# A transformer block on one core: another fixed order for the same instructions

## The chip, the cores and the metric

The kernel runs on one core of one Trainium2 chip. A core has five engines that share no clock and meet only at semaphores: TensorE (PE in the profile: matmuls; PEld: its weight loads), VectorE (DVE), ScalarE (ACT), GpSimd (POOL) and SyncE (SP), which here only issues DMAs. Each engine works off its own list of instructions in order. The metric is the time of one execution on the device in microseconds, the median of the runs.

## The reference

A pre-norm block on 2048 tokens of width 640: an attention with a compressive memory, then a feed-forward layer of width 1728.

```python
h = x + _A_ref(_layernorm(x, axis=-1), A_wq, A_wk, A_wv, A_wo, A_beta)
h2 = h + _B_ref(_layernorm(h, axis=-1), B_w1, B_w2)      # silu between the two products
...
for s in range(N):                                        # N = 4 segments of L = 512 tokens
    logits = jnp.einsum('bhqd,bhkd->bhqk', qs, ks) * scale + mask
    p = _softmax(logits, axis=-1)
    a_dot = jnp.einsum('bhqk,bhkd->bhqd', p, vs)
    num = jnp.einsum('bhld,bhde->bhle', phi(qs), M)
    den = jnp.einsum('bhld,bhd->bhl', phi(qs), z)[..., None] + 1e-06
    o = g * num / den + (1.0 - g) * a_dot
    M = M + jnp.einsum('bhld,bhle->bhde', phi(ks), vs)
    z = z + jnp.einsum('bhld->bhd', phi(ks))
```

There are 32 heads of 20 columns each. phi(t) is t + 1 for positive t and exp(t) otherwise.

## The kernel before, in words

The work is cut into four segments of 512 tokens, and each segment into tasks of one to twenty instructions. `build` declares every task with the buffers that it reads and writes and the engines that may run it. The order is not computed: a long text, `ORDER` (from L356), names every task once, and `Graph.schedule` walks it word by word. A word is `name/engine:slots`. The engine is A, D, G or S for ACT, DVE, POOL or SyncE, where the task may run on more than one; the slots are the buffers that the task is the first to use, in PSUM the first of its banks (there are eight, of 512 columns in float32). The instructions of one engine run in the order of the words. `Tracker.add` puts in the semaphore waits that reads, writes and reused buffers need. So the text fixes three things: the order on every engine, the engine of every evacuation out of PSUM, and which task reuses whose buffer.

The names, for segment s, group g of heads, column c of the projection (five of them; w = 0 for q, 1 for k):

- `x4`, `w_w1_0`: loads of tokens and weights. `re_wq0`, `re_wk0`: copies of weight columns into a padded layout (L693 on ACT, L695 on DVE).
- `n1_st`, `n1_r`, `n1_ap`: layer norm of a block of 128 tokens (statistics L743 on DVE, power L764 on POOL, scaling L770 on DVE). `n1_tp`/`n1_te`: its transpose on PE and the evacuation, for the first four blocks; `n1_tr`: the same by a DMA transpose (L799), for all others. `n2_...`: the second norm.
- `pr010x`: projection, segment 0, c = 1, w = 0, first half of the tokens (x; y is the second half) (PE, L867, the first ones L872). `qe010x`: its evacuation (ACT L883 or DVE L884). `v03`, `ve03`: V projection of a block (PE L828) and its evacuation (ACT, or DVE L843).
- `ex021`, `pha021`, `phb021`: phi, an exp on ACT (L890) and two steps on DVE (L897, L903). `kt02`, `kg02`: transpose of phi(k) by DMA and its gather. `mz10`, `ma10`: the memory's product (PE, L1226) and its addition to M (DVE L1242, in segment 0 an evacuation). `zf0`, `lsc0`: small exps of beta on ACT.
- `vt02`: copy of a part of q and k from SBUF to SBUF by DMA (L915). The five projected columns hold five groups of four heads and, in their unused rows, pieces of three more groups; twelve such copies for each segment, the virtual-head copies, put the pieces together. `vp13`: the same for phi(q). Both may be issued from SyncE's queue or from ACT's.
- `qk4x10`: scores of four heads at a time (PE, L965) into four PSUM banks. `e4x1+`: their exp on ACT in one instruction of 2048 columns (L977); `e4x30`, `e4x32` are two of 1024. `mk...`: the causal mask on POOL (L988).
- `av0x`, `oe0x`, `tn0x`, `nm0x`, `ad8`: attention times V (PE, L1093 in segment 0 and L1009 later), evacuation, transposition back (PE), normalisation on DVE, sum on POOL. `ot1`, `wo1`, `rs1`: transpose by DMA, output product (PE, L1273), residual on DVE (L1281).
- `h1_0_7_0`, `th`, `s`: first feed-forward product (PE, L1308), tanh (ACT, L1317), product (DVE, L1323). `h2_0_1`, `o0`, `out0`: second product (PE, L1350), residual (DVE, L1363), store.

The scores of the last three groups of heads (g = 5, 6, 7) read the virtual-head copies. In segment 0 `qk4x10` is the first such task: it packs group 4 with a piece of group 5, and so waits for all twelve copies `vt00` to `vt011`; `vt00`, `vt03`, `vt06` and `vt09` need columns 0, 1 and 2, the other eight columns 3 and 4. Each `vt` waits for its evacuations on the queue that issues it, and whatever comes later in that queue waits behind it.

```python
ORDER = """
...
""".split()
...
t.eng = {"A": AC, "D": DV, "G": PO, "S": SP}[eng] if eng else list(t.engs)[0]
...
virt(3 * r, allq((0, 1, 2)), QKV_[p:p + 12, :, :, :], QK_[p + 20:p + 32, 0:3, :, :])
virt(3 * r + 1, allq((3, 4)), QKV_[p + 12:p + 20, 0:2, :, :], QK_[p + 20:p + 28, 3:5, :, :])
virt(3 * r + 2, allq((3, 4)), QKV_[p + 12:p + 20, 2, :, :], QK_[p + 28:p + 32, 3:5, :, :])
```

Of the kernel before, what the change touches and what calls it, by code (L numbers as in the profile page):

```python
# [1426 lines left out]
```

## Time and profile before

| what | before |
|---|---|
| median of 3 runs | 296.63 us (296.54 to 297.4) |
| profiled execution, span from the first to the last instruction | 296.3 us (no other time is given for it) |
| ACT, DVE, POOL busy | 217.3, 222.2, 140.0 us |
| granted TensorE clock | 1.000 |
| DMA, mean over the span | 86 GB/s |
| exps of the scores on ACT (L977, 120 instructions) | 153.2 us |

A profile line of one instruction or a run of alike ones has the start in us, the length in us, the engine, the line of the code, the operation, what is written and read with its shape, the count, and in brackets the engine's idle time just before with what ended it. SPq and ACTq are DMA issues. A tile name can be that of the memory under it: segment 0 keeps its q and k in the space of `w_sb`, so its projections' evacuations and virtual-head copies read `w_sb<-ps_all` and `w_sb<-w_sb`, later segments' read QK and QKV.

### The profile page before, as it was taken

The page shows a single profiled execution, that of the slowest core. Times are in us where ns is not written, and L with a number is a line of the kernel's source. Part 1 is how long each engine was busy: PE and PEld are TensorE (multiplying, and loading weights), DVE is VectorE, ACT ScalarE, POOL GpSimd, SP SyncE. Part 2 cuts the span into 40 slices and gives each one's busy share as a digit, 9 for nine tenths or more (in the row PEclk, how much of TensorE's full clock was granted, in tenths as well). Part 3 has the DMA queues.
Part 4 walks back from the last instruction along what each step waited for, and adds up shares of the span by engine and source line. Part 5 has one row for each costly group of instructions (what it writes and reads, how often), then busy time and mean ns, then how long its engine had stood idle before and what let it go on. Part 6 is the DMA issues. An engine that isn't in the chain of part 4 may idle for free.

```text
span 296.3 us, 7415 instructions
## 1 busy us (share of the span) xinstructions
PE 282.1 (95%) x2968; PEld 167.6 (57%) x2991; DVE 222.2 (75%) x506; ACT 217.3 (73%) x266; POOL 140.0 (47%) x257
## 2 busy tenths in 40 slices
...
GB/s 243 367 173 105 173 133 71 221 18 75 189 94 74 53 60 22 40 109 106 104 96 61 66 1 2 27 76 87 22 99 32 0 61 74 68 67 25 22 22 91
DMA packets 49922, 25.40 MB, mean 86 GB/s; under 512 B 39504, under 2 KB 48048, under 8 KB 49888
## 3 DMA queue, kind: packets, MB, share of 16 engines
...
## 4 chain that ended last, share of the span: by engine, by line
PE 78%; DVE 8%; DMA 6%; issue 2%; ACT 2%; SPq 1%; POOL 1%; DVEq 0%; ACTq 0%
PE ps_all L1350 19%; PE ps_all L1308 17%; PE ps_all L867 12%; PE ps_all L965 7%; PE ps_all L1273 6%; PE ps_all L828 5%; PE ps_all L1009 5%; DMA x_tok<-in_A_x_dram 3%; DMA xT<-xn_rot 2%; ACT PT L977 2%; PE ps_all L1039 1%; DVE stt L743 1%; PE ps_all L1093 1%; DMA w_sb<-w_sb 1%; PE ps_all L1226 1%
## 5 line engine op out<-in xcount | busy, mean ns | idle before, releaser
L977 ACT ACTIVATE PT<-ps_all 128x1024 bf16<-128x1024 f32 (+1 forms) x120 | 153.2, 1310 | 16.9 <-PE ps_all L965 15.7
L988 POOL TENSOR_SCALAR_AFFINE_SELECT PT<-PT 128x512 bf16<-128x512 bf16 x128 | 81.6, 648 | 59.2 <-ACT PT L977 56.9
L1350 PE MATMUL ps_all<-w_sb,sT 128*128 128x320 bf16 (+2 forms) x462 | 64.9, 295 | 0.0
L1308 PE MATMUL ps_all<-hT,w_sb 128*128 128x512 bf16 (+1 forms) x315 | 61.0, 336 | 1.2 <-issue 0.6
L1317 ACT ACTIVATE th<-ps_all 128x512 f32<-128x512 f32 (+2 forms) x70 | 34.1, 505 | 35.3 <-PE ps_all L1308 31.2
L1350 PEld LDWEIGHTS ps_all<-w_sb,sT 128*128 128x128 bf16 x462 | 43.2, 98 | 18.3 <-issue 1.8
L1323 DVE SCALAR_TENSOR_TENSOR sT<-th,ps_all 128x512 bf16<-128x512 f32 (+2 forms) x70 | 37.9, 561 | 17.8 <-ACT th L1317 16.9
L1308 PEld LDWEIGHTS ps_all<-hT,w_sb 128*128 128x128 bf16 x325 | 29.9, 98 | 25.3 <-issue 3.5
L764 POOL TENSOR_TENSOR rst<-rst,eps_c 128x1 f32<-128x1 f32 x32 | 18.3, 576 | 24.4 <-DVE rst L758 23.1
L743 DVE BATCH_NORM_STATS2 stt<-x_tok 128x6 f32<-128x320 bf16 x62 | 27.2, 481 | 1.1 <-DMA x_tok<-in_A_x_dram 0.7
L1363 DVE SCALAR_TENSOR_TENSOR x_tok<-ps_all,x_tok 128x640 bf16<-128x640 f32 (+3 forms) x18 | 13.3, 745 | 16.7 <-PE ps_all L1350 16.6
L1071 POOL TENSOR_TENSOR otok<-on 128x320 bf16<-128x320 bf16 x24 | 19.0, 797 | 11.7 <-DVE on L1063 11.7
L1273 PE MATMUL ps_all<-wo_sb,oT 128*128 128x320 bf16 x160 | 23.8, 299 | 0.0
L884 DVE CAST QK<-ps_all 128x512 bf16<-128x512 f32 x23 | 15.7, 688 | 9.1 <-PE ps_all L867 8.9
L1063 DVE TENSOR_TENSOR on<-ps_all,rd 128x640 bf16<-128x640 f32 x24 | 19.8, 824 | 0.9
L828 PE MATMUL ps_all<-wv_sb,xT 128*128 128x320 bf16 x120 | 18.3, 299 | 1.1 <-DMA xT<-xn_rot 0.9
L1273 PEld LDWEIGHTS ps_all<-wo_sb,oT 128*128 128x128 bf16 x160 | 15.0, 98 | 7.2 <-issue 1.8
L867 PE MATMUL ps_all<-xT,wkr 128*128 128x512 bf16 x67 | 16.9, 379 | 1.2 <-issue 0.8
L867 PE MATMUL ps_all<-xT,wqr 128*128 128x512 bf16 x70 | 17.3, 380 | 0.4 <-issue 0.2
L1009 PE MATMUL ps_all<-PT,Vx 128*32 128x512 bf16 (+3 forms) x384 | 16.4, 301 | 0.1
L843 DVE CAST Vx<-ps_all 128x640 bf16<-128x640 f32 x15 | 12.3, 818 | 5.4 <-PE ps_all L828 5.3
L770 DVE TENSOR_SCALAR xn_rot<-x_tok,mvt,rst 128x640 bf16<-128x640 bf16 x32 | 14.9, 475 | 1.7 <-POOL rst L764 1.0
...
## 6 DMA issues: line engine op xcount, KB each, us to landing
...
```

Source lines behind the costliest of these rows:

```text
L743: T.add(DV, lambda e, hh=hh: e.bn_stats(out=stt[:, s, 6 * hh:6 * hh + 6], in_=xb[:, 320 * hh:320 * hh + 320]), reads=R((xa, xsub)), writes ...
L828: fns.append(lambda e, c=c, hh=hh: e.matmul(bank(ps, hh)[:, 0:320], lhsT=xT_[:, c, 128 * i:128 * i + 128], rhs=wv_sb[:, c, 320 * hh:320 * ...
L867: fns = [lambda e, kc=kc: e.matmul(bank(ps)[:, lo:hi], lhsT=wt[:, kc, c, :], rhs=xT_[:, kc, lo:hi], start=(kc == 0), stop=(kc == NC - 1)) ...
L965: fns.append(lambda e, j=j, o=o, r=r, q0=q0, q1=q1, qa=qa, ka=ka: e.matmul(ps_all[:, o:o + q1 - q0], lhsT=ka[32 * r:32 * r + DH, 128 * j:1 ...
L977: T.add(AC, lambda e: e.activation(out=pt[:, pta.slot, q0:q0 + nq, 0:width], in_=sc3[:, b0:b0 + nq, 0:width], func=ACT.Exp, scale=SCALE), ...
L988: T.add(PO, lambda e: e.affine_select(out=v, in_=v, pattern=[[0, 4], [1, 128]], compare_op=ALU.is_ge, fill=0.0, base=0, channel_multiplier ...
L1009: fns.append(lambda e, j=j, r=r, h=h, pa=pa, pt=pt, co=co, q0=q0, ji=ji: e.matmul(bank(po)[32 * r:32 * r + 32, q0:hi], lhsT=Vx[:, vx.slot, ...
L1273: fns.append(lambda e, c=c, hh=hh: e.matmul(bank(ps, hh)[:, 0:320], lhsT=oT[:, c, 128 * i:128 * i + 128], rhs=wo_sb[:, c, 320 * hh:320 * h ...
L1308: fns = [lambda e, c=c: e.matmul(bank(ps)[:, lo:hi], lhsT=w1_sb[:, c, 128 * f:128 * f + 128], rhs=hT[:, c, lo:hi], start=(c == 0), stop=(c ...
L1317: T.add(AC, lambda e: e.activation(out=th[:, tha.slot, lo:hi], in_=bank(ps)[:, lo:hi], func=ACT.Tanh, scale=0.5), reads=R((ps, [0])), writ ...
L1323: T.add(DV, lambda e: e.scalar_tensor_tensor(out=sT[:, f, lo:hi], in0=th[:, tha.slot, lo:hi], scalar=1.0, in1=bank(ps)[:, lo:hi], op0=ALU. ...
L1350: fns.append(lambda e, f=f, t0=t0, fr=fr, hh=hh, n=n: e.matmul(bank(pa, hh)[:, 0:n], lhsT=sT[:, f, t0:t0 + 128], rhs=w2_sb[:, fr, c0 + 320 ...
```

## The change

Only the text `ORDER` changes. It names the same tasks, 383 words on PE in both. On PE the order differs mainly in the first projections and scores and, at the end, in the last segment's feed-forward; in between some twenty near neighbours are swapped. On the other engines more is moved. Counted over both lists, these tasks changed their number on an engine:

| tasks | before | after |
|---|---|---|
| ve (V evacuation) | ACT 1, DVE 15 | ACT 5, DVE 11 |
| oe (attention evacuation) | ACT 9, DVE 23 | ACT 11, DVE 21 |
| qe (projection evacuation) | ACT 18, DVE 32 | ACT 19, DVE 31 |
| re_wq | ACT 1, DVE 4 | ACT 2, DVE 3 |
| ma (memory evacuation) | ACT 1, DVE 8 | DVE 9 |
| vt (virtual-head copies of q, k) | ACT 6, SyncE 42 | ACT 18, SyncE 30 |
| vp (of phi(q)) | ACT 3, SyncE 33 | ACT 11, SyncE 25 |
| out (stores) | ACT 10, SyncE 8 | ACT 13, SyncE 5 |
| kg, kh (gathers) | DVE 8, POOL 13 | DVE 9, POOL 12 |
| n1_r, n2_r (step one of the power) | DVE 16, POOL 16 | DVE 13, POOL 19 |

In segment 0 each list issues four of the twelve `vt` from ACT: before `vt07`, `vt010`, `vt00`, `vt03`, now `vt04`, `vt011`, `vt03`, `vt06`. The diff, cut to the part up to the output products wo1 and wo0 (minus lines, then plus lines), the stretch around `rs2` and `mz10`, and the end:

```diff
-epsg0:0 vpad0 zpad w2z/G:0 fill30:7 x0:0 w_q1:0 warm iota mt mta mtb mm7 x1:4 mm0 n1_st1/A:0,0 w_q0 w_q2 epsc sel
+epsg0:0 vpad0 zpad w2z/G:0 fill30:7 x0:10 w_q1:0 warm iota mt mta mtb mm7 x1:4 mm0 n1_st1/A:0,0 w_q0 w_q2 epsc sel
 halfc n1_st0/D:5 n1_r0/G n1_r1/D n1_ap0:0 n1_tp0:4 n1_te0a/A:0 n1_ap1:1 n1_tp1:0 n1_te0b/A n1_te1b/D n1_te1a/A w_k0
-re_wq1/D:0 pr010x:4 re_wq4/A re_wq2/D pr020x:2 qe020x/A:0 qe010x/A:0 re_wq3/D re_wq0/D pr000x:5 pr040x:6 w_k1
-re_wk2/A:0 qe000x/A:0 re_wk1/D qe040x/A:0 pr011x:0 qe011x/A re_wk0/D pr001x:2 pr021x:5 qe001x/A qe021x/A x2:10,5
-n1_st2/D:3 n1_r2/G qk0x10:0 pr030x:7 w_wv0:0 w_wv1 n1_st3/D:1 n1_r3/G e0x10:4 x4:2,1,11,3 qe030x/A:0 w_wo:0 beta
-w_w1_0:0 e0x12 re_wk3/D pr031x:6 n1_ap2:2 re_wk4/D x8/S:6,7,8,9 n1_ap3:0 n1_tp2:0 n1_te2/D n1_st6:4 n1_tp3:4 n1_r6/G
-n1_te3/A qe031x/D pr041x:7 qe041x/D qk0x20:0 e0x2+:6 pr030y:4 qe030y/D pr031y:5 qe031y/A pr041y:6 qe041y/A pr040y:7
-qe040y/A vt02/S:0 vt011/S vt05/S vt08/S n1_st5:1 qk0x30:0 vt04/S mk0x1_0 mk0x1_256 n1_st4:5 n1_r5/G n1_ap5:1 e0x3+:0
-n1_ap6:2 pr000y:4 qe000y/D lsc0 vt07/A pr021y:6 qe021y/D pr001y:5 qe001y/D pr011y:7 ex021:0 qe011y/D pr020y:1 n1_r4/D
-mk0x3_0 qe020y/D mk0x3_256 vt010/A pr010y:6 qe010y/D vt00/A vt03/A vt06/S v03:2 ve03/D:0 ex001:1 mk0x3_384 mk0x2_0
-v00:4 ve00/D qk0y10:0 e0y12:5 mk0x1_384 pha021:1 pha001:2 v01:6 e0y10 mk0y1_0 mk0x2_256 vt09/S phb021 vt01/S qk4x10:2
-phb001 lsc1 n1_st7:7 e4x1+:2 vpad1 v02:0 ve01/D av0x:6 mk4x1_0 n1_ap4:3 n1_r7/G qk4x20:2 e4x2+:1 n1_tr5:0 mk4x1_256
-mk4x1_384 ve02/D lsc2 lsc3 oe0x/D:0 mk4x2_0 mk4x2_256 av2x:7 ex041:1 oe2x/D:1 kt02:0 n1_tr6 mk0y1_256 mm2 kt00:1 v11:0
-qk4x30:2 e4x30:3 pha011:0 ve11/D:1 tn0x:6 nm0x:3 e4x32 mk4x3_0 pha031:1 qk0ya0:0 mk4x3_256 n1_ap7:2 mk4x3_384 v12:6
-e0ya+:4 w_w1_2 ve12/D av4x:4 oe4x/D:0 mz00:5 ma00/A:2,5 qk1ya0:0 e1ya2:0 tn2x:6 nm2x:0 av6x:7 oe6x/D:1 e1ya0 tn4x:6
-nm4x:1 qk2ya0:2 kvz e2ya2:1 tn6x:7 mm3 nm6x:2 n1_tr4 v10:0 n1_st11:2 e2ya0 qk0y20:4 e0y2+:6 w_w1_3 w_w1_1 mk0y2_0
-kg00/G:0 mk0y2_256 n1_tr7 v13:2 n1_r11/G qk3ya0:4 e3ya0:3 ve10/D n1_st9:6 n1_r9/D pha041:2 ex031:2 mm6 ve13/D ot1:0
-wo1:0 n1_st8:3 e3ya2 ot0 ex011:0 wo0:2 rs1 n2_st1:0 mk0y1_384 w_w1_4 phb011 qk4ya0:4 e4ya0:2 n2_r1/D kg02/G e4ya2 rs0
...
+re_wq1/D:0 re_wq2/D pr010x:7 pr020x:5 re_wq4/A pr040x:1 w_k1 re_wq3/D re_wq0/A pr000x:2 re_wk2/A:0 qe010x/D:0
+qe020x/A:0 qe000x/A:0 qe040x/A:0 re_wk1/D re_wk0/D pr001x:0 x2:3,0 qe001x/A pr011x:7 w_wv0:0 qe011x/A n1_st2/D:6
+n1_r2/G n1_st3/D:1 pr021x:4 qe021x/A qk0x10:0 e0x10:6 w_wv1 x4:11,5,1,6 pr030x:4 qe030x/A:0 w_wo:0 e0x12 re_wk3/D
+pr031x:7 n1_ap2:1 n1_tp2:0 beta n1_r3/G n1_ap3:2 n1_tp3:4 n1_te3/A w_w1_0:0 re_wk4/D pr041x:6 qe041x/A n1_te2/D
+qk0x20:0 e0x2+:2 qe031x/D zf0 n1_st5:5 pr041y:4 qe041y/D pha041:0 mk0x1_0 pr040y:6 x8/S:9,2,8,7 qe040y/A pr030y:5
+qe030y/D pr031y:7 qe031y/A qk0x30:1 n1_st6:6 pr020y:5 qe020y/D ex041:1 pr001y:7 qe001y/D vt08/S:0 vt05/S pr000y:5
+e0x3+:4 pha001:1 vt04/A vt011/A mk0x2_0 pr011y:7 qe011y/A lsc0 vpad1 pr021y:0 qe021y/D pha021:2 ex001:2 pr010y:4
+qe000y/D qe010y/A qk0y10:4 lsc1 e0y10:0 vt01/S n1_st7:2 vt07/S kvz phb041 n1_r6/G n1_st8:4 e0y12 ex021:1 mk0x2_256
+vt02/S n1_r5/D vt010/S n1_r7/G v03:0 ve03/A:0 phb001 phb021 n1_ap5:2 mk0x1_256 v01:2 v00:6 ve01/D vt03/A n1_ap6:3
+vt06/A vt00/S vt09/S qk4x10:2 zf1 mk0x1_384 n1_tr5:0 v02:0 ve00/A av0x:7 n1_st4:5 e4x1+:5 w_w2_4 ve02/A mk0x3_0
+mk0x3_256 qk4x20:2 mk0x3_384 mk4x1_0 mk4x1_256 n1_st9:3 lsc2 lsc3 oe0x/D:1 av2x:6 tn0x:7 nm0x:2 v11:0 mk4x1_384 mm1
+mzc1 n1_tr6 e4x2+:6 n1_r4/D mk4x2_0 mk4x2_256 oe2x/D:0 qk4x30:2 e4x30:2 e4x32 n1_ap7:1 ve11/D:1 n1_ap4:0 mk4x3_0
+mk4x3_256 kt00:0 v12:6 qk0ya0:0 e0ya+:4 ve12/D av4x:6 oe4x/D:1 w_w1_1 tn2x:7 kt02:1 ex031:1 mk4x3_384 n1_tr7 mz00:4
+ma00/D:7,3 kg00/D:0 qk1ya0:0 e1ya2:5 e1ya0 mk0y1_0 nm2x:1 av6x:5 oe6x/D:0 tn4x:6 pha031:1 qk2ya0:2 nm4x:3 mm5 mm6
+e2ya2:6 tn6x:7 nm6x:0 n1_st10:2 e2ya0 n1_tr4 v10:0 ve10/D qk0y20:4 e0y2+:3 w_w1_4 phb031 v13:2 ve13/A ot1:0 mk0y2_0
+qk3ya0:4 e3ya0:1 mk0y1_256 mk0y1_384 kg02/D n1_r8/G mm3 mk0y2_256 wo1:0 rs1 n2_st1:6 ex011:0 n2_r1/D e3ya2 ot0 wo0:2
...
-nm8:1,1 o1 kh13/G n2_r3/G ex111:2 phb111 mm1 n2_ap3:2 mk11b_0 mk11b_384 pha130:0 vt16/S mzc1 vt111/S ot2 qk12a0:2
-e12a+:0 ex140:0 mzc3 mb01:0,0 wo2:0 rs2 av10:7 oe10/D:0 phb140 ad8:0 qk12b0:2 e12b0:3 mzc5 kt12:1 mz10:0 ma10 e12b2
...
+nm8:1,0 mk10e_0 mk10e_256 e11b+:2 n2_r3/G n2_ap3:3 h2_1_3 o1 mb01:0,0 qk12a0:2 mk10a_0 phb110 mk10b_384 kt13:0
+kg13/G:0 wo2:0 kg12/G e12a+:0 av10:6 qk12b0:2 rs2 ex140:0 phb140 ad8:0 n1_tr11 mz10:0 ma10 mzc7 mk12a_0 e12b0:6
...
-h2_15_1_1 h2_15_2_1 h2_15_0_2:3 h2_15_3_1 out15_0/A o15_1 h2_15_1_2 h2_15_2_2 h2_15_3_2 o15_2 out15_2/A out15_1/S
-fill2:2
...
+h2_15_2_0 o14 out11/A out12/A out14/A h2_15_3_0 o15_0 h2_15_0_2:1 h2_15_1_2 h2_15_2_2 out15_0/A h2_15_3_2 o15_2
+out15_2/S fill2:2
```

More of the change, by code (lines that the diff above doesn't have):

```diff
@@ new lines @@
+h1_0_13_0:6 h2_0_0:4 h2_0_1 vt18/S e10a2 th0_13_0:0 ot3 mk8b_0 n1_ap10:2 ex121:0 phb121 pha131:2 mk8b_384 vt13/S
+n1_ap11:0 mk9b_0 vt110/S qk10b0:0 e10b+:3 vt15/A mk9b_384 h2_0_2 s0_13_0 av9:7 oe9/D:1 av8:6 oe8/D:0 vt10/A mzc6
+n1_tr8 n1_tr10 qk10e0:0 h2_0_3 e10e2:5 phb101 kt12:1 e10e0 vt17/S o0 h2_1_0:6 vt11/A ex131:1 phb131 qk11a0:2 e11a+:4
+wo3:0 pha130:0 h2_1_1 qk11b0:2 phb100 ex110:0 mm2 mm4 mzc2 rs3 n2_st3:1 mk10b_0 ex111:2 mzc4 mb00:0,0 tn8:0 h2_1_2
+nm8:1,0 mk10e_0 mk10e_256 e11b+:2 n2_r3/G n2_ap3:3 h2_1_3 o1 mb01:0,0 qk12a0:2 mk10a_0 phb110 mk10b_384 kt13:0
@@ new lines @@
+qe200/D:0 mk12e_256 av13:5 oe13/D:1 n2_tr3 vp15/A vp11/S vp14/S qk14b0:0 mb02:0,0,0,0 pha231:2 v23:6 ve23/D ex141:0
+n2_tr2 ad11 e14b+:1 mk14b_0 vp111/S kt10:0 mz11:4 ma11 phb231 h1_0_8_1:5 th0_8_1:0 s0_8_1 qk14e0:0 e14e+:5 vp12/S
+mk14a_0 mk12b_384 vp19/S tn13:6 h1_0_7_1:4 nm13:0,0 pr201:5 th0_7_1:1 s0_7_1 mk14b_384 qe201/A qk15a0:0 tn10:6
+pha141:0 mk14e_0 mk14e_256 e15a2:4 nm10:0,1 phb141 pr221:4 av14:5 ad13 kt14:1 av12:7 e15a0 mk15a_0 oe14/D:0 oe12/D:1
+qe221/A qk15b0:0 tn14:4 nm14:2,0 ad14 pr241:6 qe241/D:0 ex211:1 h1_0_12_1:7 e15b+:6 kg14/G mk15b_0 out0/A x12/S
```

149 lines of the change are left out of this document (70 added, 79 removed).

## The prediction, made before the run

> **What bounds the kernel now.** I read the page's first lines, then busy time by stage, then the chain of waits through the worst stage, then the instructions there in order of time. The page says that the matmuls (PE) fill the span:
>
> ```profile
> span 296.3 us, 7415 instructions
> PE 282.1 (95%) x2968; PEld 167.6 (57%) x2991; DVE 222.2 (75%) x506; ACT 217.3 (73%) x266; POOL 140.0 (47%) x257
> ```
>
> The same by stage (columns: stage, its length, then busy us of PE, PEld, DVE, ACT, POOL):
>
> ```profile
> 0.00:7.40 7.40, 5.61 (x40) 4.11 (x40) 2.53 (x8) 3.62 (x7) 4.84 (x19) 1.00 0.73 243
> 7.40:22.20 14.80, 13.16 (x154) 10.67 (x153) 13.24 (x49) 12.88 (x26) 4.49 (x11) 1.00 0.79 270
> 22.20:47.30 25.10, 21.23 (x276) 12.88 (x274) 21.20 (x48) 19.20 (x19) 17.12 (x33) 1.00 0.75 140
> 47.30:140.00 92.70, 90.02 (x1098) 52.40 (x1112) 79.03 (x190) 88.02 (x107) 54.59 (x98) 1.00 0.42 84
> 140.00:240.00 100.00, 98.07 (x1035) 52.98 (x1045) 76.72 (x161) 82.19 (x89) 55.43 (x92) 1.00 0.29 51
> 240.00:293.90 53.90, 53.74 (x377) 34.59 (x378) 29.19 (x53) 11.44 (x20) 3.51 (x7) 1.00 0.23 57
> 293.90:296.30 2.40, 0.28 (x4) 0.00 (x0) 0.29 (x1) 0.00 (x0) 0.00 (x0) 1.00 0.15 36
> ```
>
> The diff removes no matmul, so its effect is a change in PE's idle time: 1.79 us to 7.40, 1.64 to 22.20, 3.87 to 47.30, 2.68 to 140, 1.93 to 240, 0.16 to 293.9, and 2.12 in the tail. The stage from 22.2 to 47.3 has most of it for its length. From 47.3 on PE is 97 to 99% busy: a delay at 47.3 goes through to the end unless the 4.6 us of idle behind it shrink.
>
> The chain of waits through that stage:
>
> ```profile
> 22.49 0.43 DVE w_sb L884
> 22.94 0.80 SPq L915
> 23.78 0.78 SPq L915
> 24.60 3.73 DMA w_sb<-w_sb
> 28.47 0.42 PE ps_all L965 x12
> ```
>
> This is the last projection evacuation of segment 0 (qe010y, on DVE), then two of the twelve virtual-head copies on SyncE, then a third (vt01), which needs 3.73 us from issue to landing, then the first scores that read virtual heads (qk4x10). PE has nothing to do for its last 1.50 us. This is the place to follow in the new list.
>
> **The change part by part.** *Work moved.* Counting the two lists: four V evacuations (ve), net two attention evacuations (oe), one 256-wide projection evacuation and one weight copy (re_wq0) go from DVE to ACT, and one memory evacuation (ma00) goes back.
>
> ```profile
> L843 DVE CAST Vx<-ps_all x15: 773/826/828, 23.9 to 191.9; 128x640 bf16<-128x640 f32 x15
> L883 ACT ACTIVATE w_sb<-ps_all x11: 378/383/405, 10.0 to 18.8; 128x256 bf16<-128x256 f32 x11
> L883 ACT ACTIVATE QK<-ps_all x7: 589/597/618, 49.6 to 189.6; 128x512 bf16<-128x512 f32 x7
> L1022 ACT ACTIVATE oTs<-ps_all,lsc x9: 687/687/691, 114.0 to 237.5; 128x512 bf16<-128x512 f32 x9
> 10.56 0.83 ACT L693 ACTIVATE wkr<-sT 128x400 bf16<-128x400 bf16 x2
> ```
>
> No V evacuation ran on ACT. Two rows give 0.214 us per 256 elements, so 640 elements take about 0.70 us (bounds: 0.60, the 512-wide row, and 0.83, DVE's). ACT gets 4 x 0.70 + 2 x 0.69 + 0.38 + 0.83 - 0.3 = 5.1 us more, DVE about 5 us less. Neither is a sum for the end; what counts is where they stand in the chain.
>
> *Opening, to 22 us.* Here PE's order puts pr001x ahead of pr011x:
>
> ```profile
> 10.40 0.74 DVE L695 COPY wkr<-sT 128x400 bf16<-128x400 bf16 x4 [0.80 <-DMA sT<-in_A_wk_dram]
> 10.92 1.80 PE L867 MATMUL ps_all<-hT,wkr 128*128 128x256 bf16 x15
> 12.65 0.40 PE L965 MATMUL ps_all<-w_sb 20*128 20x256 bf16 x12
> 21.20 1.25 PE L867 MATMUL ps_all<-hT,wqr 128*128 128x256 bf16 x10
> ```
>
> The four copies on DVE are re_wk1 and then re_wk0. pr011x could start at 10.92, after two; pr001x needs the last, which ends at 11.14. That is 0.22 us, with some 0.06 to the release +0.28, for the scores at 12.65 and what follows. On ACT zf0 (0.22, the length of lsc0 below) and ex041 (0.63, likewise an exp of 512) come in ahead of the big exp e0x3+, and one evacuation (0.38) leaves: +0.5. e0x3+ ran from 19.12:
>
> ```profile
> 19.12 1.88 ACT L977 ACTIVATE PT<-ps_all 128x2048 bf16<-128x2048 f32 x1
> 19.24 1.62 ACTq L915 DMA_DIRECT2D w_sb<-w_sb  x1
> 20.90 0.22 ACT L638 ACTIVATE bsel<-beta_bc 128x32 f32<-128x32 bf16 x1
> 21.36 0.63 ACT L890 ACTIVATE ex<-w_sb 128x512 bf16<-128x512 bf16 x1 [0.24 <-DVE w_sb L884]
> 21.36 3.34 ACTq L915 DMA_DIRECT2D w_sb<-w_sb  x3
> 24.75 0.63 ACT L890 ACTIVATE ex<-w_sb 128x512 bf16<-128x512 bf16 x1 [2.76 <-DVE Vx L843]
> ```
>
> So now 19.12 + 0.28 + 0.5 = 19.9 to 21.8. Behind it on ACT stand qe011y, lsc0, ex001 and then qe010y: 0.38 + 0.22 + 0.63, less some overlap, so qe010y runs 23.0 to 23.4, where DVE ended it at 22.92: +0.5. PE feels this twice. In the list before two V projections (v03, v00) stood between pr010y and the scores qk0y10; now qk0y10 comes first and waits for qe010y, so v03 starts at about 23.4 + 0.40 = 23.8 (0.40 is the length of the scores at 12.65).
>
> *The virtual copies.* SyncE's eight, ACT's four (ns, smallest, median, largest) and a V projection:
>
> ```profile
> 19.23 6.07 SPq L915 DMA_DIRECT2D w_sb<-w_sb  x8
> L915 ACTq DMA_DIRECT2D w_sb<-w_sb x4: 701/860/1617, 19.2 to 23.8; - x4
> 25.44 1.53 PE L828 MATMUL ps_all<-wv_sb,hT 128*128 128x320 bf16 x10
> ```
>
> SyncE needs 0.76 each, ACT 0.86. In the new list SyncE issues six from about 19.5, then vt00 and vt09, which need qe010y: the last starts at 24.8 and lands at 28.5 by the 3.73 us above. That is no loss. But vt03 and vt06 are on ACT, in program order behind e0y10, e0y12, ex021 and ve03, and ve03 waits for v03, ready at 23.8 + 1.53 = 25.3. How far does ACT's queue issue ahead of its arithmetic? In the rows above a copy is issued at 19.24 although lsc0, ahead of it in the list, runs only at 20.90: one instruction ahead is seen. If ACT issues vt03 as soon as ve03's wait is over, it goes out at 25.3 and vt06 at 26.2. Landing: 26.2 + 3.73 = 29.9. If ve03 must first begin (e0y10 at 23.9, two exps of 1.02 by the rows below, ex021 with 0.63: 26.6), vt06 goes out at 27.5 and lands at 31.2. A lower end: the transposes' 2.7 us to landing,
>
> ```profile
> hT<-xn_rot SPq DMA_TRANSPOSE x16, 2.7
> ```
>
> gives 28.9. I take 29.9, whose landing is that of the same copy. qk4x10 moves from 28.47 to about 30.0: +1.5 (+0.5 to +2.9). [...]
>
> *From there to 47.3.* ACT is the chain: exp after exp, each waiting for the four score banks, from 28.92 to 47.75:
>
> ```profile
> 28.92 1.88 ACT L977 ACTIVATE PT<-ps_all 128x2048 bf16<-128x2048 f32 x1 [1.43 <-PE ps_all L965]
> 42.68 1.53 PE L828 MATMUL ps_all<-wv_sb,xT 128*128 128x320 bf16 x10 [0.85 <-DMA xT<-xn_rot]
> 44.59 1.02 ACT L977 ACTIVATE PT<-ps_all 128x1024 bf16<-128x1024 f32 x1 [0.84 <-PE ps_all L965]
> 47.75 1.02 ACT L977 ACTIVATE PT<-ps_all 128x1024 bf16<-128x1024 f32 x1 [0.18 <-PE ps_all L965]
> ```
>
> Into these 18.83 us the change puts ve02 and ve13 (1.40) and takes ex041 and ma00 out (0.63 + 0.31): +0.46. It also moves the transpose n1_tr7, for which v13 waited 0.85 us, ahead of all but one of the W1 loads then still open; the ACT gap of 0.84 behind that goes. If not, +0.84. Together -0.4 us: at 47.3 the kernel is 1.1 us late (0.1 to 2.5).
>
> *47 to 240.* The order on PE differs in some twenty swaps of near neighbours. One wait should go:
>
> ```profile
> 92.17 0.67 DVE L897 TENSOR_SCALAR phiQ<-QK 128x512 bf16<-128x512 bf16 x1
> 93.72 0.46 PE L1226 MATMUL ps_all<-Vx,phiKt 128*128 128x84 bf16 x8 [0.37 <-DVE x_tok L1281]
> ```
>
> The memory matmul waits for a bank that DVE's rs2 frees; the new list puts less (no pha130, that 0.67) ahead of rs2. -0.3, and with DVE 5 us lighter I take -0.5 in all (+1.0 to -2.3, half of the 4.6 us of idle). Twenty more copies are issued from ACT's queue in segments 1 to 3, twelve of them before 140. Cost zero behind an exp of 1.0 or 1.9 us, as at 19.24; without that cover 0.86 each.
>
> *The end.* PE idles 0.16 us in 53.9. The new list puts fewer second products behind wo15, whose norm the last segment's first products need: 62 matmuls in place of the 90 of this piece of the chain of waits,
>
> ```profile
> 251.69 12.22 PE ps_all L1350 x90
> ```
>
> so 8.4 us in place of 12.2. The transpose takes 2.7 of them; 5.7 are left for five steps (residual, statistics, power, scaling, o8), of which 640 columns on DVE cost 0.83 each. That covers it; each 0.1 us over would be lost. Behind the last matmul stands the same 128-column third with its store, on SyncE in place of ACT: 0.
>
> Sum: +1.5 - 0.4 - 0.5 = +0.6 on the span of 296.3. The page shows no other time for that execution; the median of the runs is 0.3 above the span, so 296.6 + 0.6 = 297.2 us. About 0.3% (0.9 us) is what a measurement of this kernel can tell from no change, so this counts as the same.
>
> **The rivals.** *Slower by the front.* ACT issues vt03 only once ve03 begins; the copies land at 31.2 and nothing behind is regained: +2.9 - 0.4 = +2.5, 299.1 us. It decides from a landing later than about 30.2. For it: 24.75 in the rows above, where an exp whose data were ready idled 2.76 us behind the three issues that end at 24.70 (the profile names a DVE task that it does not read). Against: the issue at 19.24. Chance 0.29, and 0.06 more for copies on ACT left uncovered later (four of the twelve: 3.4 us on top of a front that costs 0.1). *Faster.* The front costs only its lower end, 0.1, and the lighter DVE takes half of the idle between 47 and 240: 0.1 - 2.3 = -2.2, 294.4 us. For it: the 0.37 us at 93.72 is a wait of that kind, ended by DVE. Against: PE's order hardly changes, and ACT, 88.02 of 92.70 us busy, has no less to do. Chance 0.27. *The same*, 295.8 to 297.5: 0.38.
>
> **How the numbers follow.** The likeliest case has the sum of 297.2. The range runs from the faster case, 294.4, to the slower one, 299.1; about 2 in 10 lie outside. Faster 0.27, same 0.38, slower 0.35.
>
> **What would show it.** Right: qk4x10 starts near 30, released by the copy landing on ACT's queue; PE's wait for xT at 42.68 is gone; ACT busy about 222 us, DVE 217; the last 54 us unchanged. Wrong: qk4x10 at or before 28.5, or PE's idle time between 47 and 240 off by more than 1 us from 4.6.

## The result and the profile after

| | old list | new list |
|---|---|---|
| median, same chip | 297.01 us (296.54 to 298.79, 4 runs) | 301.77 us (301.02 to 302.82, 4 runs) |
| ratio, 95% interval | | 1.014 (1.010 to 1.018) |
| profiled execution: span, time of that execution | 296.3 us, none given | 298.9 us, 301.91 us |

The change makes the kernel slower by 4.8 us; 297.2 was forecast, with a range up to 299.1. The spans differ by only 2.6 us. Part of the answer is that the old list's profile was of a long execution: 60 later executions of the old list have a span of 295.3 us in the middle (294.7 to 297.5), and a time 1.74 us above the span (1.68 to 1.89). Another part lies behind the last instruction: the new list's profiled execution has a time 3.0 us above its span, and in its trace one last packet of the DMA queue `instruction`, 16 KB, moves from 301.25 to 302.21, where the old list's trace shows none behind its span. Why that packet comes so late isn't shown. The granted clock adds to some executions: four of ten of the new list have a mean of 0.989 to 0.994 and spans of 300.8 to 302.3, against one of the 60 old ones; the other six have 299.1 in the middle. At full clock the new list therefore costs 299.1 - 295.3 = 3.8 us by the spans, and 301.1 - 297.0 = 4.1 us by the times.

The page of the new list, its span and busy times (PE, PEld, DVE, ACT, POOL), which answer to the first fence of the prediction:

```profile
span 298.9 us, 7421 instructions
PE 282.8 (95%) x2969; PEld 167.7 (56%) x2991; DVE 219.6 (73%) x496; ACT 221.1 (74%) x274; POOL 141.1 (47%) x259
```

Its busy time by stage, in the columns of before:

```profile
7.40:22.20 14.80, 13.42 (x151) 10.42 (x152) 11.76 (x42) 13.97 (x29) 3.78 (x9) 1.00 0.81 278
22.20:47.30 25.10, 19.91 (x267) 12.13 (x266) 19.77 (x51) 20.55 (x22) 16.45 (x30) 1.00 0.57 117
47.30:140.00 92.70, 89.39 (x1082) 51.71 (x1094) 77.23 (x177) 84.84 (x102) 56.51 (x103) 1.00 0.43 88
140.00:240.00 100.00, 97.80 (x1047) 53.47 (x1048) 77.11 (x165) 86.89 (x97) 55.10 (x92) 1.00 0.33 55
240.00:293.90 53.90, 53.63 (x367) 33.73 (x369) 29.63 (x53) 11.09 (x20) 4.41 (x9) 1.00 0.20 48
```

The moved evacuations show in ACT (+3.7 us) and DVE (-2.6). PE is idle for 5.19 us from 22.2 to 47.3 (3.87 before) and 5.51 from 47.3 to 240 (4.61 before). The instructions around the first scores that read virtual heads, in order of time:

```profile
22.27 1.38 POOL L671 MEMSET phiKv<- 128x1536 bf16 x1
22.46 1.33 DVE L897 TENSOR_SCALAR phiK<-w_sb 128x512 bf16<-128x512 bf16 x1
22.55 0.38 ACT L883 ACTIVATE w_sb<-ps_all 128x256 bf16<-128x256 f32 x1
23.71 0.40 DVE L884 CAST w_sb<-ps_all 128x256 bf16<-128x256 f32 x1
24.27 0.40 PE L965 MATMUL ps_all<-w_sb 20*128 20x256 bf16 x12 [1.75 <-DVE w_sb L884]
26.18 0.84 ACTq L915 DMA_DIRECT2D w_sb<-w_sb  x1
27.05 0.81 ACTq L915 DMA_DIRECT2D w_sb<-w_sb  x1
29.98 0.40 PE L965 MATMUL ps_all<-w_sb 20*128 20x256 bf16 x12 [1.13 <-DMA w_sb<-w_sb]
```

From the top: a memset on POOL (task kvz), pha021 on DVE, qe010y on ACT, qe000y on DVE, the scores qk0y10 that wait 1.75 us for it, the copies vt03 and vt06 on ACT's queue, and qk4x10, which starts at 29.98 (30.0 was forecast). What the prediction missed stands in the second row. The same step, grouped over the old list and then over the new one (ns, smallest, median, largest):

```profile
L897 DVE TENSOR_SCALAR phiK<-w_sb x5: 282/283/398, 26.0 to 43.8; 128x512 bf16<-128x512 bf16 x5
```

```profile
L897 DVE TENSOR_SCALAR phiK<-w_sb x5: 282/293/1329, 17.7 to 56.2; 128x512 bf16<-128x512 bf16 x5
```

It takes 0.28 us, and 1.33 beside the memset: 1.05 us too long, ending 0.14 after the memset does. It reads and writes SBUF. Behind it on DVE stands qe000y, which the scores qk0y10 and the copies of columns 0 to 2 need. The second place where PE has a new wait:

```profile
124.67 0.79 POOL L1071 TENSOR_TENSOR otok<-on 128x320 bf16<-128x320 bf16 x1 [1.50 <-DVE on L1063]
124.71 0.91 DVE L897 TENSOR_SCALAR phiQ<-QK 128x512 bf16<-128x512 bf16 x1
125.42 0.69 POOL L988 TENSOR_SCALAR_AFFINE_SELECT PT<-PT 128x512 bf16<-128x512 bf16 x1
125.54 0.85 DVE L903 TENSOR_TENSOR phiK<-phiK,ex 128x512 bf16<-128x512 bf16 x1
126.31 0.41 DVE L1323 SCALAR_TENSOR_TENSOR sT<-th,ps_all 128x256 bf16<-128x256 f32 x1
126.77 1.40 PE L828 MATMUL ps_all<-wv_sb,xT 128*128 128x320 bf16 x9 [0.51 <-DVE sT L1323]
```

The new list puts pha200 and phb211 ahead of s0_6_1 on DVE; beside POOL's work they take 0.91 and 0.85 us (the medians of the same steps in this trace are 0.29 and 0.42), and v22 waits for the PSUM bank that s0_6_1 frees.

Starts of tasks on PE in us (the first weight load or matmul of each), counted from pr010x, the first projection (it starts at 8.4 to 8.7 in these five traces). The second column is the run e1_before165 below, which has the old list's words up to 165 us; its profiled execution has a span of 295.2, the old list's usual length:

| task | old list, profile shown | old list's words, later run | new list | kvz moved | kvz and s0_6_1 moved |
|---|---|---|---|---|---|
| qk0y10 | 16.42 | 16.08 | 15.78 | 14.22 | 14.22 |
| qk4x10 | 19.76 | 19.08 | 21.52 | 19.95 | 20.11 |
| qk0ya0 | 26.08 | 25.40 | 28.15 | 26.57 | 26.73 |
| pr121 | 43.94 | 42.93 | 45.84 | 44.27 | 44.42 |
| pr230 | 114.51 | 113.50 | 116.55 | 114.99 | 115.11 |
| v22 | 115.39 | 114.38 | 118.31 | 116.76 | 115.98 |
| h2_3_0 | 134.21 | 133.20 | 136.90 | 135.35 | 134.96 |

The old list's words at their usual length have qk4x10 0.7 us earlier than the profile shown, and pr121 1.0 earlier; e1_before91 below, with the old front too, has qk4x10 at 19.38. Against the usual one the new list is 2.4 us late at qk4x10, 2.9 at pr121, 3.05 at pr230, 3.9 at v22 and 3.7 at h2_3_0.

### The profile page after: what moved, and what is told of

Read it like the earlier page. It is cut to its first block, busy times and chain, and to the rows that moved or that the text cites. A ratio compares the mean times of both kernels' runs of the same rounds, so it can differ in the third digit from the quotient of the medians.

```text
span 298.9 us, 7421 instructions
## 1 busy us (share of the span) xinstructions
PE 282.8 (95%) x2969; PEld 167.7 (56%) x2991; DVE 219.6 (73%) x496; ACT 221.1 (74%) x274; POOL 141.1 (47%) x259
## 4 chain that ended last, share of the span: by engine, by line
PE 67%; ACT 12%; DVE 10%; DMA 4%; issue 3%; POOL 2%; SPq 1%; ACTq 0%; DVEq 0%
PE ps_all L1350 20%; PE ps_all L1308 13%; ACT PT L977 9%; PE ps_all L867 7%; PE ps_all L965 6%; PE ps_all L1273 6%; PE ps_all L1009 5%; PE ps_all L828 5%; DMA x_tok<-in_A_x_dram 3%; DVE stt L743 2%; ACT th L1317 2%; PE ps_all L1039 1%; DVE on L1063 1%; POOL PT L988 1%; DMA w_sb<-w_sb 1%
## 5 line engine op out<-in xcount | busy, mean ns | idle before, releaser
L1308 PE MATMUL ps_all<-hT,w_sb 128*128 128x512 bf16 (+1 forms) x316 | 60.3, 336 | 1.4 <-issue 0.8
L1317 ACT ACTIVATE th<-ps_all 128x512 f32<-128x512 f32 (+2 forms) x70 | 33.8, 508 | 35.3 <-PE ps_all L1308 26.2
L770 DVE TENSOR_SCALAR xn_rot<-x_tok,mvt,rst 128x640 bf16<-128x640 bf16 x32 | 15.8, 499 | 3.7 <-POOL rst L764 3.6
L1281 DVE TENSOR_TENSOR x_tok<-ps_all,x_tok 128x640 bf16<-128x640 f32 x16 | 12.9, 809 | 5.9 <-PE ps_all L1273 5.8
```

Of the source, the lines that this page charges most:

```text
L1308: fns = [lambda e, c=c: e.matmul(bank(ps)[:, lo:hi], lhsT=w1_sb[:, c, 128 * f:128 * f + 128], rhs=hT[:, c, lo:hi], start=(c == 0), stop=(c ...
L1317: T.add(AC, lambda e: e.activation(out=th[:, tha.slot, lo:hi], in_=bank(ps)[:, lo:hi], func=ACT.Tanh, scale=0.5), reads=R((ps, [0])), writ ...
```

## The experiments

All times are medians beside the old list's on the same chip; "span" is the middle one of the executions at full clock.

**1. Where in the list.** The new list again, two lists that follow the old one up to a point, and one with an edit in the front.

```diff
e1_before91:  the old list's words up to rs2, then the new list's order
e1_before165: the same, up to 165 us
e1_front_edit (new list):
-qk0y10:4 lsc1 e0y10:0 vt01/S
+v03:0 qk0y10:4 lsc1 e0y10:0 vt03/A vt01/S
...
-n1_st8:4 e0y12 ex021:1
+n1_st8:4 e0y12 vt06/A ex021:1
```

> The new list unchanged. In the first comparison its span grew by 2.6 us (296.3 to 298.9) and its time by 4.2 us (1.41%). Theory A (the loss is PE waiting, as in the span): ratio about 1.010, time and span apart by the same amount in both kernels. Theory B (the 25 copies issued from ACT's queue in segments 1 to 3, 5 before, cost something that the profiled span does not hold): ratio 1.014 again, time minus span about 2 us more than in the kernel before.

> The list before up to rs2 (about 91 us), the new list for all tasks behind it. It takes back the front and 3 of the 20 copies moved to ACT's queue. Theory A: the span shows +1.9 of the +2.6 us lost by then, so 0.7 us remain: ratio 1.002, at most 1.004. Theory B: the span remainder of 0.7 us and 17 of 20 copies of a further 1.6 us: ratio about 1.007.

> The list before up to qk22b0 and mz20 (about 165 us), the new list behind. In the trace the new list loses nothing more from there. Theory A: ratio 1.000. Theory B: some 7 of the moved copies lie behind 165 us, so 0.5 to 0.7 us remain: ratio 1.002.

> The new list with three words moved: v03 ahead of the scores qk0y10, vt03 on ACT directly behind e0y10 and vt06 directly behind e0y12. Both theories: the scores qk4x10 start near 28.6 in place of 29.98, and PE's waits of 1.75 us before qk0y10 and 1.13 us before qk4x10 shrink to 0.5 us or less each. Theory A: the 1.3 us go through to the end, ratio 0.0045 below that of the unchanged new list. Rival to it: ACT, over 90% busy from 47 to 140 us, is the bound there, and half or more of the gain is lost again: ratio at most 0.002 below.

| run | median, us | ratio to the old list | span |
|---|---|---|---|
| e1_again | 302.31 | 1.0178 (1.0143 to 1.0213) | 299.3 |
| e1_before91 | 297.94 | 1.0039 (1.0022 to 1.0056) | 296.1 |
| e1_before165 | 298.04 | 1.0032 (1.0017 to 1.0048) | 296.2 |
| e1_front_edit | 301.03 | 1.0132 (1.0115 to 1.0148) | 299.15 |

At full clock 3.0 of the 3.8 us come from the order up to 91 us (299.1 against 296.1). The two mixed lists don't divide the other 0.8: e1_before165, which neither theory saw above 1.002, loses as much as e1_before91. At its seam each also runs tasks in an order that neither whole list has, and what that costs was not tested. Theories A and B both miss: the ratio of the unchanged list is 1.018 and not 1.010, and its time is within 0.1 us of 1.74 above the span in five of the ten executions and 2.0 to 3.4 above it in the other five. The front edit looks like the gain of 0.0045 that was expected, but its span says otherwise: its four executions were all at full clock, three of the six of the new list were not. In its trace qk4x10 came 0.6 us earlier counted from pr010x (20.93) and qk0ya0 0.1 later (28.25): won and lost again. PE's wait ahead of qk4x10, which was to shrink to 0.5 us, grew from 1.13 to 1.65. The ratio that was expected came for the wrong reason.

**2. The memset, the evacuations behind it, the second wait, and the queue.**

```diff
e2_kvz_early:
-qe011y/A lsc0 vpad1
+qe011y/A kvz lsc0 vpad1
...
-vt07/S kvz phb041
+vt07/S phb041
e2_pha_late:
-qe021y/D pha021:2 ex001:2 pr010y:4 qe000y/D qe010y/A qk0y10:4
+qe021y/D ex001:2 pr010y:4 qe000y/D qe010y/A pha021:2 qk0y10:4
e2_s06_early:
-pha211:0 pha200:0 phb211 h1_0_5_1:4 s0_6_1
+pha211:0 s0_6_1 pha200:0 phb211 h1_0_5_1:4
e2_vt_sync:
-vt03/A n1_ap6:3 vt06/A
+vt03/S n1_ap6:3 vt06/S
```

> The new list with one word moved: kvz, the 1.38 us memset on POOL, goes ahead of lsc0, into POOL's idle time before 22 us. In the new kernel's trace pha021 on DVE takes 1.33 us at 22.46, beside that memset (22.27 to 23.65), where the same step takes 0.28 elsewhere; qe000y, the last evacuation before qk0y10 and before the copies vt00, vt03, vt06 and vt09, stands behind it. Theory L (DVE and POOL block each other on this step): pha021 back at about 0.29, qk0y10 and qk4x10 about 1.05 us earlier counted from pr010x (14.75 and 20.5 in place of 15.8 and 21.5), the time about 1.0 us less than the new list's, ratio to the kernel before about 1.009 to 1.010. Theory Q (the copies vt03 and vt06 are late since they stand on ACT's queue behind two exps): qk0y10 moves, qk4x10 stays at 21.2 or later, ratio unchanged at 1.013 to 1.018.

> The new list with pha021 moved behind qe000y and qe010y; the memset kvz stays where it was. Theory L: the step may still be stretched, but behind the evacuations, so that qk0y10 comes 1.3 us earlier counted from pr010x (14.45) and qk4x10 about 1.0 to 1.3 earlier (20.2 to 20.5); ratio to the kernel before about 1.008 to 1.010. Theory Q: qk4x10 stays at 21.2 or later and the ratio at 1.013 to 1.018.

> The new list with s0_6_1 moved two words up on DVE, ahead of pha200 and phb211, which took 0.91 and 0.85 us at 124.7 to 126.4 beside POOL's ad15 and mk16a (0.28 and 0.42 elsewhere). It frees the PSUM bank that v22 waits for. Theory M (v22's wait of 0.51 us is a loss to the end): the wait goes, the time is 0.4 to 0.5 us less than the new list's, the way from pr230 to v22 1.26 in place of 1.77. Rival N: PE only waits a little further on, since the 0.16 to 0.3 us waits behind it are set by ACT's exps: no change of the time over 0.1 us.

> The new list with vt03 and vt06 put on SyncE's queue, which then issues vt03, vt06, vt00 and vt09 one behind the other, 0.82 us each from 24.2 on; on ACT's queue nothing is left behind the exps. Theory Q (ACT's queue is what makes the copies late): the last issue ends at 27.5 in place of 27.86, qk4x10 0.4 us earlier or more; ratio 0.001 to 0.002 lower. Theory L (the copies are late since qe000y is late): the last lands at 29.6 to 30.4, between 0.3 us earlier and 0.5 us later than in the new list, ratio within 0.002 of it.

| run | median, us | ratio to the old list | span |
|---|---|---|---|
| e2_kvz_early | 300.58 | 1.0101 (1.0067 to 1.0135) | 297.75 |
| e2_pha_late | 300.23 | 1.0084 (1.0053 to 1.0115) | 297.8 |
| e2_s06_early | 301.05 | 1.0121 (1.0093 to 1.0150) | 299.05 |
| e2_vt_sync | 302.05 | 1.0159 (1.0125 to 1.0194) | 298.5 (one execution) |

With the memset earlier, in order of time:

```profile
18.40 1.38 POOL L669 MEMSET phiKv<- 128x1536 bf16 x1
19.13 0.97 DVE L882 CAST w_sb<-ps_all 128x256 bf16<-128x256 f32 x2
21.92 0.29 DVE L895 TENSOR_SCALAR phiK<-w_sb 128x512 bf16<-128x512 bf16 x1
22.13 0.42 DVE L882 CAST w_sb<-ps_all 128x256 bf16<-128x256 f32 x1
22.70 0.40 PE L963 MATMUL ps_all<-w_sb 20*128 20x256 bf16 x12 [0.72 <-DVE w_sb L882]
28.40 0.40 PE L963 MATMUL ps_all<-w_sb 20*128 20x256 bf16 x12 [1.13 <-DMA w_sb<-w_sb]
```

pha021 is back at 0.29 us. qk0y10 and qk4x10 come 1.56 and 1.57 us earlier from pr010x, more than the 1.05 expected, and the span is 1.35 us shorter. The two evacuations at 19.13 take 0.97 us beside the memset, and the same two take 0.97 in the new list with POOL idle: these two, which read PSUM, are not held up. With the memset left and the step moved behind the evacuations:

```profile
22.13 1.38 POOL L670 MEMSET phiKv<- 128x1536 bf16 x1
22.55 1.11 DVE L896 TENSOR_SCALAR phiK<-w_sb 128x512 bf16<-128x512 bf16 x1
22.86 0.40 PE L964 MATMUL ps_all<-w_sb 20*128 20x256 bf16 x12 [0.48 <-ACT w_sb L882]
```

The step is still stretched, to 1.11 us, but nothing waits for it: qk4x10 at 20.16, span 297.8. Two different edits cure the same delay by the same amount, so theory L holds here for DVE's step. That POOL is held up too isn't shown: its memset takes 1.38 us in each of these traces. Moving the copies to SyncE did not help: qk4x10 at 22.00 in a trace disturbed by the clock (experiment 4), and its one execution at full clock 0.6 us below the new list's. That run can't tell Q from L; the two others do. s0_6_1 earlier takes v22's wait away:

```profile
126.59 1.52 PE L827 MATMUL ps_all<-wv_sb,xT 128*128 128x320 bf16 x10
```

v22's first weight load comes 0.89 us earlier from pr010x, its first matmul 0.7, and h2_3_0 0.51, as theory M has it. The times don't show it: the intervals of this run and of the new list overlap, and the span, of two executions at full clock, is 0.05 below.

**3. The clash put into the old list, both cures together, and the copies once more.**

```diff
e3_before_clash (old list): kvz from behind qk2ya0:2 to directly ahead of n1_r4/D
e3_both: the edits of e2_kvz_early and e2_s06_early
e3_mend: e3_both, and
-e0y10:0 vt01/S
+e0y10:0 vt03/A vt06/A vt01/S
```

> The kernel before with one word moved: kvz, the memset on POOL, goes ahead of n1_r4, into POOL's idle time at 19.4 to 21.7 us; there DVE does n1_ap5 and n1_ap6 (0.44 us each), with the projection evacuations and so the virtual-head copies behind them. Theory L (DVE's SBUF step and POOL's memset block each other): n1_ap5 or n1_ap6 takes 1.2 to 1.4 us longer, all later evacuations and copies move by that, qk4x10 comes at 20.3 to 21.1 from pr010x in place of 19.1 to 19.8, the time rises by 1.0 to 1.4 us, ratio 1.0035 to 1.005. Theory Q (only the order of the evacuations and the queue of the copies matter; POOL was idle there): ratio 1.000, qk4x10 unmoved.

> The new list with both words moved, kvz ahead of lsc0 and s0_6_1 ahead of pha200. If the two losses add (1.5 us at qk4x10 and 0.5 us at v22 in the single runs), h2_3_0 on PE comes 2.0 us earlier than in the new list counted from pr010x (134.9 in place of 136.9), 1.7 us later than in the kernel before at its usual speed (133.2); ratio to the kernel before 1.006 to 1.008. If one hides the other: 1.008 to 1.010.

> The kernel of the run with both words moved, and besides vt03 and vt06 directly behind e0y10 on ACT, in place of behind e0y12, ex021 and ve03. Theory Q in what is left (the two copies on ACT's queue hold qk4x10 up): their last issue ends at about 22.8 to 24.8 us in place of 26.3, qk4x10 comes 0.5 to 0.8 us earlier and the end with it; ratio 1.004 to 1.006. Rival D: DVE is behind at oe0x, 3 us later, and the gain is lost again ahead of tn0x, as when the copies were moved alone (0.6 us won at qk4x10, 0.7 lost at qk0ya0): ratio as with both words, 1.006 to 1.008.

| run | median, us | ratio to the old list | span |
|---|---|---|---|
| e3_before_clash | 297.92 | 1.0037 (1.0025 to 1.0049) | 296.2 |
| e3_both | 298.77 | 1.0090 (1.0061 to 1.0119) | 296.75 |
| e3_mend | 300.92 | 1.0140 (1.0126 to 1.0154) | 298.95 |

One word of the old list, a memset put into an idle stretch of POOL, costs 0.9 to 1.0 us. Its trace:

```profile
19.30 1.38 POOL L670 MEMSET phiKv<- 128x1536 bf16 x1
19.39 1.82 DVE L769 TENSOR_SCALAR xn_rot<-x_tok,mvt,rst 128x640 bf16<-128x640 bf16 x2
28.57 0.40 PE L964 MATMUL ps_all<-w_sb 20*128 20x256 bf16 x12 [1.41 <-DVE mvt L745]
```

and the same two scalings in the old list's profile:

```profile
19.85 0.80 DVE L770 TENSOR_SCALAR xn_rot<-x_tok,mvt,rst 128x640 bf16<-128x640 bf16 x2
```

n1_ap5 and n1_ap6 take 1.82 us in place of 0.80, and qk4x10 starts at 20.17 from pr010x in place of 19.08 to 19.76. (The step mvt that the profile names as the end of its wait is none that the scores read; the last copy landed at 28.36, 0.2 us ahead.) So the clash is shown alone, in both lists, and cured in two ways.

Both cures together give h2_3_0 at 134.96 (134.9 expected) and a span 2.35 us below the new list's. The ratio of 1.009, above the 1.006 to 1.008 expected, holds two executions of six at a clock of 0.994; the four others have 298.5 us. What is left at full clock is 1.45 us.

The copies ahead of e0y12 on ACT (theory Q for the rest) made it worse by 2.2 us:

```profile
24.34 1.70 ACTq L913 DMA_DIRECT2D w_sb<-w_sb  x2
26.08 1.02 ACT L975 ACTIVATE PT<-ps_all 128x1024 bf16<-128x1024 f32 x1 [0.72 <-issue]
27.65 0.86 DVE L901 TENSOR_TENSOR phiK<-phiK,ex 128x512 bf16<-128x512 bf16 x1 [1.21 <-ACT ex L888]
30.03 0.26 PEld L963 LDWEIGHTS ps_all<-w_sb 20*128 20x128 bf16 x12 [1.68 <-DMA w_sb<-w_sb]
30.07 0.40 PE L963 MATMUL ps_all<-w_sb 20*128 20x256 bf16 x12 [1.38 <-DVE Vx L841]
```

The issues hold ACT's second exp back by 0.72 us; ex021 behind it is late, so phb021 on DVE falls beside POOL's masks and takes 0.86 us, and qk4x10 now waits for ve01 on DVE, done at 29.92; it comes 0.85 us later than with both cures (20.96). The last copy, though issued 0.9 us earlier from pr010x, landed at 29.71, 4.5 us after its issue began (3.0 with both cures), so without ve01 too the scores would have come late. At tn0x there is a further wait of 1.32 us. Theory Q falls: an earlier issue did not bring an earlier landing. Rival D named the right engine, but the gain at qk4x10 that it expected to be lost later did not come at all.

**4. The clock.** In e2_vt_sync, the 3.41 us ahead of the clock's fall, and the 3.41 us at the lower clock (us of PE, PEld, DVE, ACT, POOL, then granted clock):

```profile
22.38:25.79 3.41, 1.67 (x24) 1.09 (x22) 3.28 (x7) 1.58 (x4) 2.93 (x5) 1.00 0.25 43
25.79:29.20 3.41, 3.41 (x15) 1.94 (x14) 2.22 (x8) 2.40 (x4) 2.11 (x4) 0.50 0.56 82
```

PE worked for 1.67 of 3.41 us, and then had half its clock for 3.41 us. Traces of e2_pha_late and e4_front2 show such a stretch from 41.0 and 40.8 us, behind the short waits from 36 us on; in e2_pha_late PE had worked for 2.29 of the 3.41 us ahead of it. Dummy matmuls in PE's waits, in the new list and in the one with both cures:

```diff
e3_fills (new list), e4_both_fills (e3_both, with fill6 for fill14):
+fill14:0 ahead of qk0y10:4, fill9:0 ahead of qk4x10:2, fill3:4 ahead of av4x:6,
+fill5:7 ahead of qk2ya0:2, fill3:7 ahead of qk3ya0:4
```

> The new list with 34 dummy matmuls of 256 columns into free PSUM banks in five of PE's waits (before qk0y10, qk4x10, av4x, qk2ya0 and qk3ya0); nothing else is changed. In executions of the new list and of lists near it, some show a stretch of 3.41 us at a granted clock of 0.50 at 25.8 or 41.0 us, and the mean clock of the execution is then 0.994 and its span 1.3 to 2.5 us longer; the kernel before showed none. Theory C (PE's waits in the front let the clock drop): with the waits filled the mean clock is 1.00 in all executions, the median is that of the new list's undisturbed executions, about 301.0, ratio 1.012 to 1.014. Rival: the dips have nothing to do with PE's waits; a third to a half of the executions keep a clock of 0.994 and the ratio is 1.013 to 1.018.

> The kernel with both words moved, with 26 dummy matmuls in five of PE's waits. With both words moved and no dummies, two of six executions had a mean clock of 0.994 and were 1.3 to 2.8 us longer than the other four. Theory C (PE's waits let the clock drop): all executions at 1.00, median 298.5 to 299.0, ratio 1.005 to 1.007. Rival (the dips don't come from these waits): again a third of the executions at 0.994, highest near 301.

e3_fills: 301.09 us, ratio 1.0146 (1.0131 to 1.0160), all four executions at a clock of 1.00. e4_both_fills: 299.27 us, 1.0069 (1.0050 to 1.0088), all six at 1.00, the longest 299.75. Without dummies 6 of 16 executions of the same two lists (new: 4 of 10; both cures: 2 of 6) were below 0.995. That speaks for theory C. It doesn't settle it: e1_front_edit and e3_mend had no such execution in four each, without dummies. The dummies themselves lengthen the span by 0.8 us in e4_both_fills, so that they shorten only the long executions.

**5. The rest at qk4x10, and the copies of the old list.**

```diff
e4_front2: e3_both, and
-qe010y/A qk0y10:4
+qe010y/A phb041 v03:0 ex021:1 vt03/A vt06/A qk0y10:4
e4_before_vt01 (old list): vt01/S behind vt09/S becomes vt01/A behind vt010/A
```

> The kernel with both words moved (kvz, s0_6_1), and besides, directly ahead of qk0y10, what stands ahead of it or ahead of its exps in the list before: v03 on PE, ex021 and the copies vt03 and vt06 on ACT (and phb041, whose buffer ex021 reuses). What is left of the loss with both words moved is 1.0 us at qk4x10 and 0.6 behind it. Theory F (PE has nothing to do while it waits for the last evacuation, and the copies wait behind exps): qk4x10 at 19.1 to 19.6 from pr010x in place of 20.1, h2_3_0 at 134.0 to 134.4 in place of 134.96; time 0.5 to 1.0 us below the kernel with both words moved, ratio to the kernel before 1.002 to 1.004. Rival W (a new wait takes its place, as when only the copies were moved: there phb021 and n1_ap5 on DVE ran beside POOL's masks, and qk4x10 waited for ve01): qk4x10 at 20.0 or later, ratio 1.005 or more.

> The kernel before with one copy moved: vt01 goes from SyncE's queue, where it is the last one issued (24.07 us), to ACT's directly behind vt010, where ACT's queue is free from 21.64 to 22.41 and its inputs are evacuated. Theory T (qk4x10 waits for the copy that is issued last): the last issue ends at 24.07 in place of 24.76, and qk4x10 comes 0.3 to 0.7 us earlier (18.4 to 18.8 from pr010x in place of 19.1 to 19.8); ratio 0.9977 to 0.999. Rival B (the copies that are in flight together share their time, so the last one lands when it did): qk4x10 within 0.15 us, ratio 1.000. Rival S (ACT's next exps start later, as when copies were moved ahead of them): ratio 1.001 or more.

e4_front2: 299.89 us, ratio 1.0101 (1.0065 to 1.0137), span 297.4, 0.65 above e3_both's. PE's wait ahead of qk0y10 is gone, and this stands in its place:

```profile
24.94 1.94 ACT L975 ACTIVATE PT<-ps_all 128x1024 bf16<-128x1024 f32 x2 [1.09 <-PE ps_all L963]
26.93 1.53 PE L826 MATMUL ps_all<-wv_sb,hT 128*128 128x320 bf16 x10 [1.28 <-ACT PT L975]
```

v00 waits 1.28 us for the bank that the later exps free; qk4x10 comes at 20.06, no earlier than with both cures. Rival W.

e4_before_vt01: 297.03 us, ratio 0.9998 (0.9980 to 1.0016). The last issue ends at 24.14 in place of 24.76 (e1_before165), and the last copy lands no earlier, at 27.65 in place of 27.45. From the chain of waits:

```profile
23.31 4.34 DMA w_sb<-w_sb
27.90 0.43 PE ps_all L964 x12
```

So theory T falls. The copy of the chain is vt03 (72 KB), 4.34 us from issue to landing; vt06, of the same size, took 2.88 in the new list, where the four copies of this size go out over 3.7 us in place of 1.7. That fits rival B, copies in flight together share their time; no run changes this alone. No version tried here beats the old list.

## Why the prediction was wrong

In the two profiles, counted from pr010x (0.25 us earlier in the new list), the way to qk4x10 grew by 1.8 us, from there to pr121 by 0.1, to h2_3_0 by 0.8 and to the end by 0.2; +1.5, -0.4, -0.5 and 0 were forecast. So two gains that were counted on did not come, and the costs that the runs show (a memset and a mask beside VectorE's steps) stood in no term.

*The front, to qk4x10: +1.5.* The start at 30.0 came out at 29.98, by two errors that cancel. The step "qe010y runs 23.0 to 23.4 ... qk0y10 comes first and waits for qe010y" failed: ACT had qe010y done at 22.93, and qk0y10 waited for qe000y on DVE until 24.1, since pha021 ahead of it was stretched by the memset. So vt03 and vt06 were issued at 26.18 and 27.05 in place of 25.3 and 26.2 (that ACT's queue issues vt03 as soon as v03 is ready held here: v03 starts at 24.60 and takes 1.53 us, vt03 goes out at 26.18, ve03 runs only at 27.06). The landing that was taken as 3.73 us took 2.9 from the issue of vt06, 2.08 from that issue's end.

The memset's move was in the diff, on an engine that is 47% busy, and it got no price: that is the step of this term that failed, and it cost 1.35 us at full clock (experiment 2). The step on DVE ended 0.14 us behind the memset, 1.05 us late (0.15 us behind it in e2_pha_late, where it began 0.42 us after the memset), and two PSUM evacuations beside the memset took 0.97 us in e2_kvz_early, as without it. The traces show the delay beside the memset, and not what in the chip causes it. One reading of the prediction was wrong and changes no sum: a V evacuation did run on ACT in the old list, 0.73 us at 164.93.

*From there to 47.3: -0.4.* This gain failed. The wait for xT went as forecast, but qk0ya0 is 0.3 us further behind qk4x10 than before, and smaller waits came: the new list has 0.59, 0.35, 0.66 and 0.48 us between 37 and 45.5. To pr121 it gained nothing (+0.1 against the profile shown, +0.5 against the usual execution).

*47 to 240: -0.5.* This is the term that failed outright. The wait of 0.37 us ahead of the memory's product went as forecast, and DVE was 2.6 us lighter over the whole span, but the order on it put two SBUF steps ahead of s0_6_1, beside POOL's work: at v22 alone that cost 0.7 us (its first matmul comes 1.77 us behind pr230's, 1.09 in the old list), and from pr121 to h2_3_0 the new list is 0.8 us longer. With s0_6_1 moved 0.4 to 0.5 of it went.

*The base.* "The median of the runs is 0.3 above the span" joined two different executions. The profiled one had a span 1.0 us above the usual 295.3, and the time stands 1.74 above a span. In spans the sum thus began 1.0 us too high (the old list's own late copy counted as normal); from span to time it took 0.3 where 1.74 is usual. Of the 4.7 us between 297.2 and the 301.91 of the profiled execution, 2.0 are the span's terms, 1.4 are this step, and 1.3 lie behind the last instruction.

*The clock* had no term. Four of ten executions lost another 1.7 to 3.2 us to it. *The end: 0* was right. The slower rival had the sign and the place, not the cause: the copies landed at 29.9 and not at 31.2, and moving vt03 and vt06 in three ways (e1_front_edit, e2_vt_sync, e3_mend) brought nothing. The signs of being right nearly all came true (qk4x10 at 29.98 behind a copy on ACT's queue, no wait for xT, ACT at 221.1, the end unchanged; only DVE's 219.6 stands off 217), and PE's idle time between 47 and 240 moved by 0.9 us, inside the limit of 1. So they could not tell this outcome from the forecast.

In sum, of 3.8 us at full clock, the memset's clash is 1.35 and both cures together are 2.35; 1.45 is left, 0.7 to 1.0 of it at qk4x10 by the traces. The parts don't add up well: s0_6_1's move is worth 0.05 alone, 1.0 on top of the memset's, and 0.4 to 0.5 in the traces. The rest is not settled: each edit there put another wait in the place of the one it removed. That 3.0 of the 3.8 lie in the order up to 91 us suggests, and doesn't show, that most of the rest comes from the evacuations, copies and exps of the front together; the 0.9 us of e1_before165, which has the old order at v22, has no explanation.
